# Two chunks' seeds in one pass, the last filter constants in a reused buffer, and new planner numbers, in an FFT convolution beside a Fourier mixing layer

## The chip, the cores and the metric

The kernel runs on one core of a Trainium2 chip. The core has a matrix engine (PE; its weight loads are listed as PEld), a vector engine (DVE), a scalar engine (ACT), a general engine (POOL) and an engine that here only issues DMAs (SP). The metric is the time of one execution in microseconds (us). Times inside the profile count from the first instruction of its span.

## The reference

Two independent layers read different inputs, and their outputs are put side by side, 2048 rows by 512 + 512 columns.

```python
# A: Fourier mixing, x is 2048 x 512
a = x @ dft_hid_re.T ; b = x @ dft_hid_im.T
ya = dft_seq_re @ a - dft_seq_im @ b
# B: a diagonal state space layer as a long convolution, u is 2048 x 512, 128 states for each of 512 channels
dt = exp(log_dt); A = -exp(log_A_real) + 1j * A_imag; C = (C_real + 1j * C_imag) * dt
K[d, l] = 2 * Re(sum_n C[d, n] * exp(A[d, n] * dt[d] * l))      # l = 0..2047
yb = causal_convolution(u, K) + u * D_skip                      # written with rfft / irfft of length 4096
```

## The kernel before: how the work is tiled and what sets its order

All instructions are recorded by Python generators, one for each piece of work. A small planner (`Plan`) keeps a time for each engine and records next whatever can start first by its own costs; between equals the smaller urgency number goes first. A `yield "dve", cost` in the code is one such piece; `Sem` and `Event` stand for buffers and for results. So a cost or an urgency in the code does not slow or speed anything by itself: it sets the order in which instructions stand in the engines' queues, and each engine then works its queue strictly in that order.

Layer A (class `Fnet`). The sequence matrices are streamed in as 32 quads ("S", 1 MB each, `load_quad`): a base tile and three others, which DVE combines into `rest` (L414), ACT squares for a guard value (L443) and PE multiplies (L520, L523). After each of four groups PE multiplies by the hidden matrices (L619, L620) and ACT and SP take `out_ya` away (L645, L648). `GROUP_US` and `QUAD_US` give the earliest planned time at which each quad may be asked for: "the pace of S". When the last quad is done, `spare` hands its two `slots` to layer B as further buffers.

Layer B (class `Ssm`), in stages that overlap:

- Seeds. For a chunk of 32 channels, `seed_args` makes 11 powers' exponents and angles: five small ACT copies (L993, L995), two DVE operations (L997, L999), then Abs, Exp and three Sin on ACT (L1001 to L1009). Exp and Sin live in different ACT tables, so each pass has ACT_TABLE_LOADs. `seeds` multiplies them on DVE (L1018) into the chunk's `cs` tile, of which there are two. The tile `seed` exists once.
- Tables. For each of the 16 chunks DVE doubles two tables of powers: `tables1` (T1, L944 and L953, 32 entries) and `tables2` (T2, L944 to L1110, with ACT squares in the tile `square`, L960, L967). This is most of DVE's work.
- Taps. PE multiplies the two tables into 96 numbers for each channel (`taps`, L1158), ACT moves them into `ks` (L1182).
- First FFT stage of K (`stage1_k`, L1234) for each two chunks, stored to DRAM in four tensors `xk`; the last two chunks (`last_stage1_k`, L1206) go to SBUF by DVE transposes (L1212) instead, with their own copy of the constants (`f1k_last`, L1283).
- Products. The channels fall into five units: 0, 1, 2 of 128 channels (four quarters each), 3 and 4 of 64 (two each). For a quarter, the spectra `xu` of u and `xk` of K are loaded from DRAM into a big buffer (L1367), PE does the second stage (L1399), ACT moves it out (L1424; unit 4: L1414), DVE multiplies (four operations, L1429 and L1431; unit 4: L1417), PE does the first inverse stage (L1445), ACT copies it (L808) and it is stored as `zs` (L796). Unit 3 is in `LATE`: its DVE products wait for chunk 15's T1 in the plan. Unit 4 stays in SBUF: four more transposes on DVE (L1496).
- Inverses. `zs` of a whole unit is loaded again (L1504), PE does the last stage (L1516), ACT or DVE copies, and `out_yb` is stored.

The buffers that products and inverses share are three `big` tiles, two `mid` tiles, later the two `slots`, and after chunk 15's tables the memory of the tables themselves (`more`). PE has four PSUM tiles (f0 to f3).

## Time and profile before

| what | value |
|---|---|
| three runs | 486.59, 488.81 and 490.38 us; median 488.81 |
| the profiled execution | 487.21 us |
| its span, first to last instruction | 485.10 us, so 2.11 us lie around it |
| busy in the span | PE 397.4, DVE 428.5, ACT 347.4 us |
| granted TensorE clock, mean | 0.961 |

A row of the timeline gives start, duration, engine, line and operation, out<-in, the shape and a count; a bracket says how long the engine stood idle just before and what ended that. "issue" in such a bracket means that nothing the profile shows was waited for. A row of the windows gives each engine's busy time in one stretch, then the granted clock, the share of the DMA engines and their rate. The end of T1 of a chunk is the end of its last L953.

### The profile page before, as it was taken

To read this page: it belongs to the slowest core of one execution; us is meant where nothing else is said; L and a number is where in the kernel's file an instruction comes from. 1 tells how busy PE (TensorE), PEld (TensorE's weight loads), DVE (VectorE), ACT (ScalarE), POOL (GpSimd) and SP (SyncE) were. 2 spreads that over 40 slices of the span, in tenths; PEclk is the share of its full clock that TensorE was granted. 3 is DMA by queue.
4 is the path that set the end of the run, shared out by engine and by line. 5 is a ranking of instruction groups with operands and counts; after the bars stand their busy time and mean duration, and the time that the engine had idled before them with its cause. 6 is when DMAs were issued, how large, how long until landed. Compare 5 with 4: busy or idle time off the path is not lost. (4 is left out here: it accounts for less than half of the span.)

```text
span 485.1 us, 13793 instructions
## 1 busy us (share of the span) xinstructions
PE 397.4 (82%) x5744; PEld 213.3 (44%) x5778; DVE 428.5 (88%) x732; ACT 347.4 (72%) x687; POOL 1.3 (0%) x15
## 2 busy tenths in 40 slices
PE   4548958999998695798897799998976989886593
PEld 3113214354534352453445254644343556665383
DVE  3999997989999999989999999999999999982433
ACT  1529899899998884669858988887897754633331
POOL 1000000000000000000000000000000000000000
PEclk9988987999999998999999999999999999997888
DMA  8998894895976379994986279449301995998674
GB/s 308 340 295 297 291 330 139 295 329 189 278 281 214 139 204 322 336 286 154 284 258 235 61 232 309 141 119 329 87 3 49 251 296 165 288 253 195 220 198 112
DMA packets 130546, 110.49 MB, mean 228 GB/s; under 512 B 57136, under 2 KB 101552, under 8 KB 129968
## 3 DMA queue, kind: packets, MB, share of 16 engines
q1 hardware_dynamic: 122512, 106.55, 70.1%
q10 hardware_dynamic: 7968, 3.02, 2.4%
q8 instruction: 47, 0.77, 0.7%
q14 instruction: 19, 0.16, 0.1%
HBM read 77.11 MB, written 32.44 MB: 226 GB/s over the span
## 5 line engine op out<-in xcount | busy, mean ns | idle before, releaser
L944 DVE TENSOR_TENSOR prod<-tables,cs 128x1024 f32<-128x1024 f32 (+4 forms) x160 | 124.6, 798 | 3.7 <-ACT tables L1087 2.3
L619 PE MATMUL f<-p,w 128*128 128x512 f32 x128 | 67.7, 610 | 8.9 <-ACT y L645 5.8
L953 DVE TENSOR_TENSOR tables<-prod 128x512 f32<-128x512 f32 (+4 forms) x160 | 74.0, 477 | 0.8
L443 ACT ACTIVATE slots<-rest 128x1536 f32<-128x1536 bf16 x32 | 47.4, 1480 | 16.3 <-DVE rest L414 13.8
L414 DVE TENSOR_TENSOR rest<-slots,base 128x512 bf16<-128x512 f32 (+2 forms) x52 | 53.8, 1034 | 1.9 <-DMA slots<-in_sT 1.8
L1158 PE MATMUL f<-tables 128*32 128x96 f32 x2048 | 47.0, 247 | 9.2 <-ACT big L808 2.8
L1158 PEld LDWEIGHTS f<-tables 128*32 128x32 f32 x2048 | 42.6, 110 | 18.6 <-issue 6.0
L520 PE MATMUL f<-base,es 128*128 128x512 f32 x64 | 36.9, 660 | 15.5 <-ACT es L331 7.2
L1110 DVE TENSOR_TENSOR tables<-tables,cs 128x1024 f32<-128x1024 f32 x32 | 38.0, 1220 | 0.0
L619 PEld LDWEIGHTS f<-p,w 128*128 128x128 f32 x128 | 22.5, 189 | 32.0 <-issue 16.0
L520 PE MATMUL f<-base,ec 128*128 128x512 f32 x64 | 34.3, 618 | 1.2 <-ACT big L1424 0.8
L523 PE MATMUL f<-rest,xi 128*128 128x512 bf16 x87 | 26.2, 397 | 5.7 <-ACT xi L273 2.5
L1399 PE MATMUL f<-big,w 64*32 64x256 f32 (+1 forms) x768 | 23.7, 380 | 6.1 <-DMA big<-xk 5.1
L1424 ACT ACTIVATE big<-f 128x1024 f32<-128x1024 f32 x22 | 21.9, 1020 | 7.8 <-PE f L1399 3.9
L808 ACT ACTIVATE big<-f 128x512 f32<-128x512 f32 x39 | 21.0, 588 | 7.2 <-PE f L1516 7.2
L523 PE MATMUL f<-rest,xr 128*128 128x512 bf16 x92 | 25.2, 379 | 0.6 <-DVE rest L414 0.4
L967 ACT ACTIVATE tables<-tables 128x1024 f32<-128x1024 f32 x16 | 16.8, 1050 | 10.5 <-PE f L1158 8.4
L1234 PE MATMUL f<-ks,f1k 32*128 32x512 f32 (+1 forms) x224 | 22.4, 499 | 2.3 <-ACT ks L1182 1.5
L523 PEld LDWEIGHTS <-xi 128*128 128x128 bf16 x96 | 9.5, 101 | 30.1 <-issue 21.8
L520 PEld LDWEIGHTS f<-base,es 128*128 128x128 f32 x64 | 11.8, 203 | 24.6 <-ACT es L331 10.5
L1023 ACT ACTIVATE cs<-cs 128x352 f32<-128x352 f32 x32 | 15.8, 530 | 9.0 <-DVE cs L1018 8.9
L1399 PEld LDWEIGHTS f<-big,w 64*32 64x32 f32 x768 | 14.0, 111 | 15.9 <-issue 10.6
(187 smaller groups left out, 732.7 us busy)
## 6 DMA issues: line engine op xcount, KB each, us to landing
slots<-in_sT SPq DMA_DIRECT2D x31, 768.0 KB, 6.0
xu<-big SPq DMA_DIRECT2D x16, 512.0 KB, 4.1
base<-in_sT SPq DMA_DIRECT2D x31, 256.0 KB, 6.2
xk<-big SPq DMA_DIRECT2D x7, 1024.0 KB, 6.8
big<-xu SPq DMA_DIRECT2D x11, 512.0 KB, 7.7
big<-xk SPq DMA_DIRECT2D x11, 512.0 KB, 7.3
zs<-mid SPq DMA_DIRECT2D x10, 512.0 KB, 6.2
big<-zs SPq DMA_DIRECT2D x10, 512.0 KB, 7.0
```

What stands on the lines that cost most here:

```text
L414: return v.tensor_tensor(rest[:, lo:hi:step], raw[:, lo:hi:step], base[:, None, :].to_broadcast([128, n, DM]), op=op)
L443: nc.scalar.activation(raw, rest, AF.Square, accum_out=self.stat[:, n:n + 1])
L520: nc.tensor.matmul(out, x[:, cols], base, start=k == 0, stop=False)
L523: nc.tensor.matmul(out, still[:, cols], rest[:, h], start=False, stop=k == 3 and h == 2)
L619: nc.tensor.matmul(ps, self.w[k][:, cols], self.p[t, c][:, d], start=k == 0, stop=False)
L944: self.nc.vector.tensor_tensor(p.rearrange("p k d c m -> p k (d c) m"), src.rearrange("p d c l -> p (d c) l")[:, None, :, rows].to_broadca ...
L953: self.nc.vector.tensor_tensor(dst[:, :, :, rows], p[:, 0], p[:, 1, :, ::-1], op=OP.add)
L1110: self.nc.vector.tensor_tensor(self.top[:, :, k, ::1 - 2 * k, 16:32], t[:, :, :, 1:32:2], cs[:, k, 5, :, :, None].to_broadcast([128, CHUNK ...
L1158: nc.tensor.matmul(ps[32 * j:32 * j + 32, i], t1[:, d, c], t2[:, :, d, c], start=c == 0, stop=c == 1, tile_position=(0, 32 * j))
L1234: nc.tensor.matmul(to, self.f1k[r, STEPS[a]], taps, start=a == 0, stop=a == 4, tile_position=(32 * j, 0))
L1399: nc.tensor.matmul(both[:, :, c], self.w2[rows, R * q + r, xx, 32 * c:32 * c + 32], xs[rows, r, xx], start=True, stop=True, tile_position= ...
L1424: a.activation(flat[:, 1024 * m:1024 * m + 1024], p.rearrange("p b d -> p (b d)"), AF.Copy)
```

## The change

1. Seeds are made for chunk 0 alone, for chunks 1 and 2, 3 and 4, ... 13 and 14 together, and for chunk 15 alone (`PAIRS`): nine passes in place of 16. A pass over two chunks has the same ten ACT operations and two DVE operations on 704 columns instead of 352. `seed` and the two `par` tiles become twice as large; the parameters of a pair come in one DMA (7 loads instead of 14 on SP). The DVE multiply into `cs` stays one for each chunk.
2. `f1k_last` no longer has its own 1.5 KB for each partition: it takes the tile `square`, and so its ACT copy waits for the new event `squared`, set after the last use of the squares in chunk 15's T2. The loads of unit 4's `xu` come behind that copy.
3. Numbers for the planner: urgency of the seeds 0.5 to 1.5 and of their arguments 0.3 to 1 (both still ahead of the tables' 2 and more, now behind taps and K stage with 0.5); taps cost 2.8 instead of 2.45; `GROUP_US` 42 to 41 and `QUAD_US` 11 to 8.
4. `spare` counts its buffers from `SLOTS`; with `SLOTS` = 2 it hands over the same one big and one mid tile.

```diff
-ARGS = 0.3
+ARGS = 1
...
+    def take_pair(self, g):
+        first, m = PAIRS[g]
+        self.pair[g] = self.tab.tile([128, 4, 2 * CHUNK], F32, name="par", bufs=2)[:, :, :m * CHUNK]
+        for j in range(m):
+            self.par[first + j] = self.pair[g][:, :, CHUNK * j:CHUNK * j + CHUNK]
...
-        self.par[ck] = self.tab.tile([128, 4, CHUNK], F32, name="par", bufs=2)
-        o = CHUNK * ck - FIRST
-        yield "dma", load(2 * CHUNK)
-        self.nc.sync.dma_start(self.par[ck], self.par_dram[:, :, o:o + CHUNK])
+        self.take_pair(g)
+        first, m = PAIRS[g]
+        o = CHUNK * first - FIRST
+        yield "dma", load(2 * m * CHUNK)
+        self.nc.sync.dma_start(self.pair[g], self.par_dram[:, :, o:o + m * CHUNK])
...
-        s = self.tab.tile([128, 3, 11, CHUNK], F32, name="seed")
+        s = self.tab.tile([128, 3, 11, 2 * CHUNK], F32, name="seed")[:, :, :, :w]
...
-        n = 11 * CHUNK
-        yield "act", 1.49
+        n = 11 * w
+        yield "act", 0.95 + 2 * n * 0.00085
...
-    def seeds(self, ck, s):
+    def seeds(self, g, j, s):
         yield self.css
+        s = s[:, :, :, CHUNK * j:CHUNK * j + CHUNK]
...
-        self.plan.put(self.res)
+        if j == PAIRS[g][1] - 1:
+            self.plan.put(self.res)
...
-        for n in range(16):
-            box, ev = args[n]
+        for g, (first, m) in enumerate(PAIRS):
+            box, ev = args[g]
             yield ev
-            if n < 15:
-                self.plan.spawn(self.seed_args(n + 1, *args[n + 1]), ARGS)
-            self.cs[n] = yield from self.seeds(n, *box)
-            self.plan.set(self.cs_ev[n])
+            if g < len(PAIRS) - 1:
+                self.plan.spawn(self.seed_args(g + 1, *args[g + 1]), ARGS)
+            for j in range(m):
+                self.cs[first + j] = yield from self.seeds(g, j, *box)
+                self.plan.set(self.cs_ev[first + j])
...
-            self.plan.put(self.pars)
+            if any(n == first + m - 1 for first, m in PAIRS):
+                self.plan.put(self.pars)
...
+            if n == 15:
+                self.plan.set(self.squared)
...
-            yield "pe", 2.45, None, 257
+            yield "pe", 2.8, None, 257
...
-        self.f1k_last = self.tab.tile([128, 3, 128], F32, name="f1k_last")
+        yield self.squared
+        self.f1k_last = self.tab.tile([128, 512], F32, name="square")[:, :384].rearrange("p (e s) -> p e s", e=3)
...
+PAIRS = ((0, 1), *((n, 2) for n in range(1, 15, 2)), (15, 1))
-FIRST_TABLE, T1, SEEDS = 0.01, 0.005, 0.5
+FIRST_TABLE, T1, SEEDS = 0.01, 0.005, 1.5
-GROUP_US, QUAD_US, AHEAD_US = 42, 11, 25
+GROUP_US, QUAD_US, AHEAD_US = 41, 8.0, 25
```

Since the planner's numbers change, nearly every queue is in another order. Three places matter below. Lines of the changed kernel are 12 to 20 higher: L944, L953, L1158, L1206, L1212, L1399, L1429, L1431, L1445 and L1516 of before are L956, L965, L1176, L1224, L1230, L1418, L1448, L1450, L1464 and L1535 after; L1367, L1504 and L796 are L1386, L1523 and L799.

First, DVE at the end of chunk 15's tables. Before, its queue reads (from the last steps of T2; the two rows of 128x32x16 on `tables<-prod` close the halves of T1 of chunk 15):

```order
L1106 SCALAR_TENSOR_TENSOR tables<-tables 128x32x16
L1110 TENSOR_TENSOR tables<-tables,cs 128x64x16
L1110 TENSOR_TENSOR tables<-tables,cs 128x32x2x16
L953 TENSOR_TENSOR tables<-prod 128x32x16
L944 TENSOR_TENSOR prod<-tables,cs 128x1024
L953 TENSOR_TENSOR tables<-prod 128x32x16
L1429 TENSOR_TENSOR mid_106<-slots 128x512
L1212 STREAM_TRANSPOSE tables<-f_4486 128x2x8x32
L1431 TENSOR_TENSOR slots<-slots 128x2x256
L1212 STREAM_TRANSPOSE tables<-f_4487 128x2x8x32
L1429 TENSOR_TENSOR mid_106<-slots 128x512
L1431 TENSOR_TENSOR slots<-slots 128x2x256
```

After, the corresponding stretch of the same queue starts a little ahead of T2's last step; ten rows with T1's smaller steps and two transposes (L1230) stand between its end and the second fence:

```order
L1448 TENSOR_TENSOR slots<-big_102 128x512
L1450 TENSOR_TENSOR big_102<-big_102 128x2x256
L1124 SCALAR_TENSOR_TENSOR tables<-tables 128x32x16
L1128 TENSOR_TENSOR tables<-tables,cs 128x64x16
L1128 TENSOR_TENSOR tables<-tables,cs 128x32x2x16
L956 TENSOR_TENSOR prod<-tables,cs 128x128
L965 TENSOR_TENSOR tables<-prod 128x64
L1448 TENSOR_TENSOR mid_105<-slots 128x512
L1450 TENSOR_TENSOR slots<-slots 128x2x256
L1448 TENSOR_TENSOR mid_105<-slots 128x512
L1450 TENSOR_TENSOR slots<-slots 128x2x256
```

```order
L956 TENSOR_TENSOR prod<-tables,cs 128x1024
L965 TENSOR_TENSOR tables<-prod 128x32x16
L1448 TENSOR_TENSOR mid_106<-big_103 128x512
L1450 TENSOR_TENSOR big_103<-big_103 128x4x128
L1448 TENSOR_TENSOR mid_106<-big_103 128x512
L1450 TENSOR_TENSOR big_103<-big_103 128x4x128
L1448 TENSOR_TENSOR slots<-big_104 128x512
L1450 TENSOR_TENSOR big_104<-big_104 128x4x128
L1448 TENSOR_TENSOR slots<-big_104 128x512
L1450 TENSOR_TENSOR big_104<-big_104 128x4x128
L1230 STREAM_TRANSPOSE tables<-f_4690 128x2x8x32
L1230 STREAM_TRANSPOSE tables<-f_4697 128x2x8x32
```

Moved: the products of unit 2's last two quarters (eight operations) and two of the four transposes now stand between the ends of T1 of chunk 14 and of chunk 15, before they stood behind; behind T1 of chunk 15 there now follow at once the products of unit 3.

Second, PE around chunk 15's taps (`L1158` / `L1176` x64 is one chunk). Before, from these taps on:

```order
L1158 MATMUL f_4527<-tables 32x96 x64
L1206 MATMUL f_4553<-ks,f1k_last 128x256 x2
L1206 MATMUL f_4588<-ks,f1k_last 128x256 x2
L1206 MATMUL f_4553<-ks,f1k_last 128x256 x2
L1206 MATMUL f_4588<-ks,f1k_last 128x256 x2
L1206 MATMUL f_4553<-ks,f1k_last 128x8x16 x2
L1206 MATMUL f_4588<-ks,f1k_last 128x8x16 x2
L1206 MATMUL f_4553<-ks,f1k_last 128x8x16 x2
L1206 MATMUL f_4588<-ks,f1k_last 128x8x16 x2
L1206 MATMUL f_4553<-dskip,f1k_last 128x8 x2
L1206 MATMUL f_4588<-dskip,f1k_last 128x8 x2
L1399 MATMUL f_4626<-big_103,w_95 32x2x128 x16
```

After, up to these taps (`L622` and `L623` are layer A's last products, before L619 and L620):

```order
L1418 MATMUL f_4612<-big_104,w_95 32x2x64 x32
L1418 MATMUL f_4613<-big_104,w_95 32x2x64 x32
L622 MATMUL f_4568<-p_3462,w_504 128x512
L623 LDWEIGHTS v_552
L623 MATMUL f_4568<-low_3497,v_552 128x512
L622 MATMUL f_4568<-p_3462,w_582 128x512
L623 LDWEIGHTS v_607
L623 MATMUL f_4568<-low_3497,v_607 128x512
L622 MATMUL f_4568<-p_3879,w_307 128x512
L623 LDWEIGHTS v_405
L623 MATMUL f_4568<-low_3897,v_405 128x512
L1176 MATMUL f_4615<-tables 32x96 x64
```

Moved: the second stage of unit 2's last quarter and of both quarters of unit 3 stood behind the last taps and now stands ahead of them; layer A's last products, which before were done ahead of the taps of chunk 14, now stand behind those: six pairs of them between the taps of chunks 14 and 15, three behind the taps of chunk 15.

Third, SP's queue of transfers near the end. Before (`xu` and `xk_86` 128x16x64 are the loads for units 3 and 4, `zs_89` is unit 2's store):

```order
L1367 DMA big_103<-xu 128x8x128
L1367 DMA big_103<-xk_85 128x8x128
L1367 DMA big_102<-xu 128x16x64
L1367 DMA big_102<-xk_86 128x16x64
L796 DMA out_yb<-big_104 128x4x128
L1367 DMA tables<-xu 128x16x64 x2
L1269 DMA tables<-in_ibl 128x2048
L1367 DMA tables<-xu 128x16x64
L1367 DMA tables<-xk_86 128x16x64
L796 DMA zs_89<-mid_106 128x8x128
L796 DMA zs_89<-slots 128x8x128
L1504 DMA big_104<-zs_89 128x1024 x2
```

After:

```order
L799 DMA xk_86<-big_104 128x2048
L799 DMA zs_89<-mid_106 128x8x128
L1386 DMA big_103<-xu 128x16x64
L1386 DMA big_103<-xk_86 128x16x64
L651 DMA out_ya<-y 128x512
L1386 DMA tables<-xu 128x16x64
L1386 DMA big_104<-xu 128x16x64
L1386 DMA big_104<-xk_86 128x16x64
L799 DMA zs_89<-slots 128x8x128
L1386 DMA tables<-xu 128x16x64
L799 DMA zs_89<-mid_105 128x8x128
L1523 DMA big_102<-zs_89 128x1024
```

Moved: both quarters of unit 3 are loaded into `big` tiles, ahead of unit 2's last stores; before, the second quarter (`tables<-xk_86`) waited for the tables' memory, behind the 1 MB load of `in_ibl`. The `big` tiles are free because unit 1's inverse loads (`zs_88`) and its `out_yb` stores now stand ahead of the loads for unit 2.

More of the change, by code (lines that the diff above doesn't have):

```diff
@@ L456, in spare @@
         flat = self.slots_all.rearrange("p n h t -> p (n h t)")
-        self.ssm.give_tile(self.ssm.big, flat[:, :2048])
-        self.ssm.give_tile(self.ssm.mid, flat[:, 2048:])
+        n = 3 * DM * SLOTS // 2048
+        for m in range(n):
+            self.ssm.give_tile(self.ssm.big, flat[:, 2048 * m:2048 * m + 2048])
+        for m in range(2 * n, 3 * DM * SLOTS // 1024):
+            self.ssm.give_tile(self.ssm.mid, flat[:, 1024 * m:1024 * m + 1024])
     def first(self):
@@ L736, in __init__ @@
         self.kss, self.res = Sem(1), Sem(1)
-        self.t1_half, self.half_taps, self.last_xt, self.last_k, self.last_ib = (Event() for _ in range(5))
+        self.t1_half, self.half_taps, self.last_xt, self.last_k, self.last_ib, self.squared = (Event() for _ in range(6))
         self.k_left = 2
@@ L845, in load_tables @@
         rest = part[4][:, :4 * (DM - FIRST)].rearrange("p (a d) -> p a d", a=4)
-        first = self.tab.tile([128, 4, CHUNK], F32, name="par", bufs=2)
+        first = self.tab.tile([128, 4, 2 * CHUNK], F32, name="par", bufs=2)[:, :, :CHUNK]
         yield self.pars
+        self.pair = {0: first}
         self.rest, self.par = rest, {0: first}
@@ L913, in setup_rest @@
         yield self.pars
-        self.par[1] = self.tab.tile([128, 4, CHUNK], F32, name="par", bufs=2)
-        yield "act", act(4 * CHUNK)
-        self.nc.scalar.activation(self.par[1], par[:, :, :CHUNK], AF.Copy)
+        self.take_pair(1)
+        yield "act", act(8 * CHUNK)
+        self.nc.scalar.activation(self.pair[1], par[:, :, :2 * CHUNK], AF.Copy)
         self.plan.set(self.par1_ev)
@@ L1001, in seed_args @@
         a.activation(k, r, AF.Abs)
-        yield "act", 1.74
+        yield "act", act(n) + 1.36
         a.activation(e, e, AF.Exp, scale=-1.0)
-        yield "act", 1.57
+        yield "act", act(6 * w) + 1.32
         a.activation(r[:, 0:6], r[:, 0:6], AF.Sin, scale=TWO_PI)
-        yield "act", act(5 * CHUNK)
+        yield "act", act(5 * w)
         a.activation(r[:, 6:11], r[:, 6:11], AF.Sin, scale=-TWO_PI)
@@ L1031, in tables @@
         yield from self.setup()
-        args = [([], Event()) for _ in range(16)]
+        args = [([], Event()) for _ in PAIRS]
         self.plan.spawn(self.seed_args(0, *args[0]), ARGS)
```

14 lines of the change are left out of this document (7 added, 7 removed).

## The prediction

> **What bounds the kernel now.** I read the busy totals first, then the windows by stage, what DVE waited for, and last the timelines of DVE, PE and SP near the end. The totals of the page:
>
> ```profile
> PE 397.4 (82%) x5744; PEld 213.3 (44%) x5778; DVE 428.5 (88%) x732; ACT 347.4 (72%) x687; POOL 1.3 (0%) x15
> q8 instruction: 47, 0.77, 0.7%
> ```
>
> DVE is the fullest engine, but the windows say where. They are cut at the ends of T1 of chunk 14 (call it T14) and of chunk 15 (T15); the columns are PE, PEld, DVE, ACT and POOL busy, then the granted clock:
>
> ```profile
> 60.00:140.00 80.00, 71.64 (x610) 31.48 (x612) 75.09 (x132) 76.11 (x152) 0.00 (x0) 0.94 0.80 263
> 140.00:412.09 272.09, 234.56 (x3395) 125.25 (x3421) 263.27 (x457) 211.90 (x418) 0.00 (x0) 0.99 0.66 204
> 412.09:425.78 13.69, 11.65 (x372) 8.69 (x368) 13.35 (x21) 8.37 (x15) 0.00 (x0) 1.00 0.98 281
> 425.78:485.10 59.32, 40.56 (x1256) 32.20 (x1256) 25.79 (x36) 18.78 (x31) 0.00 (x0) 0.86 0.74 195
> ```
>
> From 60 us to T14 DVE is idle for 4.9 + 8.8 = 13.7 us of 352: there the time is DVE's work. In the last 59.3 us DVE is 43% busy and PE 68%: no engine is full, a chain is long. So two numbers decide: T14, and the 485.1 - 412.1 = 73.0 us behind it. DVE's longest waits:
>
> ```profile
> DVE prod L1429 <- ACT tables L1424: 10.1, 1, 10.1
> DVE prod L944 <- ACT tables L1087: 2.3, 1, 2.3
> ```
>
> The first is in the tail, the second the longest between 60 us and T14. DVE's timeline gives the marks:
>
> ```profile
> 411.42 0.67 DVE L953 TENSOR_TENSOR tables<-prod 128x512 f32<-128x512 f32 x1
> ...
> 425.09 0.69 DVE L953 TENSOR_TENSOR tables<-prod 128x512 f32<-128x512 f32 x1
> ...
> 430.10 2.07 DVE L1212 STREAM_TRANSPOSE tables<-f 128x512 f32<-128x512 f32 x2
> ```
>
> T14 is 411.42 + 0.67 = 412.09, T15 is 425.09 + 0.69 = 425.78. PE's timeline, with the price of each step that I use:
>
> ```profile
> 401.25 1.13 PE L619 MATMUL f<-p,w 128*128 128x512 f32 x2
> 402.21 0.38 PE L620 MATMUL f<-low,v 128*128 128x512 bf16 x1
> 402.52 1.96 PE L1399 MATMUL f<-big,w 64*32 64x256 f32 x64
> ...
> 415.22 2.85 PE L1158 MATMUL f<-tables 128*32 128x96 f32 x128
> ...
> 428.33 1.61 PE L1206 MATMUL f<-ks,f1k_last 32*128 32x256 f32 x32 [0.67 <-ACT ks L1182]
> ...
> 431.89 1.23 PE L1445 MATMUL f<-slots,ia 32*64 32x256 f32 x26
> ...
> 434.13 0.85 PE L1399 MATMUL f<-big,w 64*32 64x128 f32 x39
> ...
> 442.11 1.56 PE L1445 MATMUL f<-slots,ia 32*64 32x256 f32 x21 [3.69 <-issue]
> ...
> 447.44 2.59 PE L1399 MATMUL f<-tables,w 64*32 64x128 f32 x165
> ...
> 457.72 2.00 PE L1445 MATMUL f<-prod,ia 32*64 32x256 f32 x28 [2.92 <-issue]
> 460.45 1.98 PE L1516 MATMUL f<-big,ib 128*64 128x128 f32 x16 [0.73 <-ACT prod L808]
> 462.36 3.08 PE L1399 MATMUL f<-tables,w 64*32 64x128 f32 x128
> ...
> 469.42 1.18 PE L1445 MATMUL f<-tables,ia 32*64 32x256 f32 x32
> ```
>
> A pair of layer A's products takes 402.52 - 401.25 = 1.3 us, a first inverse stage 434.13 - 431.89 = 2.2. Unit 3's second quarter, out of the tables' memory, comes only at 447.44; unit 4's last second stage at 462.36; its last first inverse stage starts at 469.42, and from there copies, transposes, last stage and store take 485.10 - 469.42 = 15.7 us to the end.
>
> **The change part by part.** Sums are made against the profiled execution's 487.21 us (span 485.10); the median of the runs is 1.60 us higher, which I add at the end.
>
> *Seeds in pairs, ACT.* Rows by shape, and a wide copy as the price of a wide operation:
>
> ```profile
> L1005 ACT ACT_TABLE_LOAD x16 | 20.5, 1283 | 0.2
> L1003 ACT ACT_TABLE_LOAD x15 | 19.2, 1283 | 0.3
> L1003 ACT ACTIVATE seed<-seed 128x352 f32<-128x352 f32 x16 | 7.9, 497 | 0.2
> L1182 ACT ACTIVATE ks<-f 128x768 f32<-128x768 f32 x8 | 6.4, 797 | 0.5 <-PE f L1158 0.5
> ```
>
> ACT's queue has 18 table loads in place of 32: 14 x 1.283 = 18.0 us less. Seven passes of ten operations go, and one twice as wide costs at most 0.80 instead of 2 x 0.50: about 0.2 x 70 = 14 us more. ACT falls from 347 to about 315 us. DVE's work covers this: ACT's relief shows only where DVE waited, so the ends are 0 and -13.7; I take 0, since no wait of DVE there is above 2.3 us. The Trainium skill (ScalarE: Activation LUTs, "What ACT_TABLE_LOAD costs") gives 2.66 us for a switch with its drain. By that ACT would be spared 37 us by the switches alone; the rows show 1.283 us and no drain.
>
> *Seeds in pairs, DVE.*
>
> ```profile
> L999 DVE TENSOR_TENSOR seed<-seed x16: 511/520/527, 41.0 to 378.6; 128x352 f32<-128x352 f32 x16
> L1018 DVE TENSOR_TENSOR cs<-seed x16: 885/890/899, 50.2 to 388.4; 128x704 f32<-128x704 f32 x16
> ```
>
> At 704 columns L999 costs what L1018 does, 0.89 instead of 1.04; for L997 I take the same saving. 7 x 0.30 = 2.1 us, half of it if only the overlap-free part counts. I take -1.5, all on the path to T14.
>
> *Seeds less urgent, par loads.* `seed` exists once: a pair's arguments start when the pair before is multiplied out, and then have about a chunk's time (366 us from 60 to T15 for 16 chunks, 23 each) for ten ACT operations of at most 0.8 us and two loads, 10.6 us. So I take 0; ends 0 and +5 (half a microsecond of hungry DVE in each pass). SP's seven par loads less are hidden by the same slack.
>
> *DVE between T14 and T15.* Eight product operations and two transposes are added here (first order fences):
>
> ```profile
> L1431 DVE TENSOR_TENSOR big<-big 128x512 f32<-128x512 f32 x22 | 15.2, 692 | 1.5
> L1212 DVE STREAM_TRANSPOSE tables<-f 128x512 f32<-128x512 f32 x4 | 4.2, 1092 | 0.0
> ```
>
> 8 x 0.69 + 2 x 1.09 = 7.7, less overlap about 7.2. T15 goes from T14 + 13.7 to T14 + 20.9; the second added transpose ends some 6 us ahead of that, at + 15.
>
> *PE behind T14.* Its new queue, in us from T14: taps of chunk 14 to 2.9, a pair of layer A 4.2, unit 2's last second stage 6.2, a first inverse stage 8.4, L1206 (1.9 with its small rows) 10.3, unit 3's first quarter (2.3) 12.6. The next first inverse stage needs the PSUM tiles of the two transposes: 15 to 17.2. Two pairs 19.8, unit 3's second quarter 22.1, three pairs 26.0, taps of chunk 15 28.9. So T15 is not on the path any more: PE comes five microseconds later. Copy into `ks`, a pair and L1206 to 32, transposes to 34; unit 3's two first inverse stages, with a pair between, to 39; its copies and an inverse piece (1.0) to 41; unit 4's first quarter (2.6, between 2.0 and 3.1) 43.7, two inverse pieces 45.7, its second quarter 48.4; an inverse piece, a first inverse stage and unit 3's inverse (1.2) to 52.8. There unit 4's last first inverse stage starts, 15.7 us before the end: 68.5.
>
> *Pauses.* PE's pauses marked "issue" are in none of these steps; before, they cost 3.69 and 2.92 in the stretch where unit 2's and 3's steps stood close. 47 pieces of code serve 5744 + 5778 = 11,522 instructions, about 250 each, and the new stretch is as dense. I take +2, ends 0 and +7. The Trainium skill (Runtime: NRT & Kernel Launch, "Instruction fetch mechanics") says that crossing a block of 256 instructions is mostly hidden. By that this term would be 0; the two pauses speak against it.
>
> So 73.0 us become 70.5: -2.5, ends -4.5 and +2.5. Most of what unit 3 gains by its `big` tiles is paid back by layer A's nine pairs (11.5 us) that now stand behind T14.
>
> *The wait for `squared`.* Behind the ACT copy stand the copies of unit 2's last product. The squares are used up 3 us behind T14, as the taps end, and that product comes at 6.2: 0, at most 1 without this cover.
>
> *The pace of S* gave these places; by itself I put 0, between -3 and +3.
>
> Sum: 485.1 - 1.5 - 2.5 = 481.1, with 2.1 around it 483.2, and 1.6 for the median: **484.8 us**.
>
> **Rivals.** *C, ACT's relief counts.* If half of DVE's 13.7 us of idle time goes, T14 and the end come 7 us earlier: 478. For it: ACT is 95% busy in 60:140, and DVE idles there. Against: the waits are many and short.
>
> *A, pauses and round trips eat the rest.* Unit 2's spectrum goes through DRAM before its inverse, and PE's queue stands behind that inverse.
>
> ```profile
> 445.24 0.36 SPq L796 DMA_DIRECT2D zs<-slots  x1
> 450.41 1.69 SPq L1504 DMA_DIRECT2D slots<-zs  x2
> ```
>
> Before, from the last store (445.24) to the inverse (460.45) it took 15.2 us. Now the store is due at T14 + 18.5, its loads behind an `out_ya` store that waits for layer A's pairs (+26.5): the inverse may come at +45 instead of +40. 484.8 + 5 = 490, no change.
>
> *B, slower: the last K spectrum comes late.* Unit 3's products now stand ahead of chunk 15's taps in PE's queue. If `xk_86` has not landed, PE stops, and all behind it.
>
> ```profile
> 414.27 0.33 SPq L796 DMA_DIRECT2D xk<-big  x1
> xk<-big SPq DMA_DIRECT2D x7, 1024.0 KB, 6.8
> big<-xk SPq DMA_DIRECT2D x11, 512.0 KB, 7.3
> ```
>
> Before, the product ran 434.13 - 414.27 = 19.9 us after the store was issued, at T14 + 22.0. Now PE is there at + 10.3; landing at + 22 would cost 12: 497 us. Against it: the K stage stands two stages, three pairs (8 us) ahead of chunk 14's taps in the new queue, so its copies (3), store and load are done by T14 + 9. It makes the change slower by over 1% from a landing at T14 + 20 on.
>
> **How the numbers follow.** My forecast (480 to 489) has 0.50, C 0.20, A 0.16, B 0.14. Within 1% of the median, about what a measurement of this kernel can tell from no change, is 484 to 494. Faster: C and under half of the forecast, 0.42; same: the rest of it and A, 0.43; slower: B and an edge, 0.15. The range 474 to 496 leaves out the lower part of C and the upper half of B.
>
> **What would show it.** DVE near full up to T14, and T14 between 408 and 413; ACT near 315 us with 17 or 18 table loads; no DMA wait of PE at unit 3's second stage; chunk 15's taps some 5 us behind T15; 68 to 73 us from T14 to the end. A T14 below 406 would be C, a wait for `zs` at L1535 A, a DMA wait at L1418 ahead of the taps B.

## The result and the profile after

| | before | changed |
|---|---|---|
| median of 20 runs, us | 488.96 (485.45 to 492.97) | 485.76 (482.87 to 494.11) |
| profiled execution, us | 487.21 | 486.11 |
| its span, us | 485.10 | 484.30 |
| granted TensorE clock, mean | 0.961 | 0.937 |

The ratio changed / before is 0.9937, 95% interval 0.9909 to 0.9965: 0.6% faster, within the 1% named as "same". Ratios here and below are taken over undisturbed runs alone, so they need not equal the quotient of the medians, which are over all runs.

The totals of the changed kernel's page, and the rows of its ACT table loads:

```profile
PE 403.1 (83%) x5737; PEld 212.0 (44%) x5778; DVE 426.8 (88%) x718; ACT 320.9 (66%) x603; POOL 1.3 (0%) x15
```

```profile
L1017 ACT ACT_TABLE_LOAD x9 | 11.5, 1283 | 0.1
L1015 ACT ACT_TABLE_LOAD x8 | 10.3, 1283 | 0.1
```

ACT lost 26.6 us and has 17 of these loads left (and one at L331). DVE lost 1.7. PE is 5.7 us busier for the same 5778 weight loads, at a lower granted clock. The marks on DVE's timeline (start, duration; T14 ends with the first of the two operations of the first row):

```profile
409.77 1.02 DVE L965 TENSOR_TENSOR tables<-prod 128x512 f32<-128x512 f32 x2
...
431.01 0.69 DVE L965 TENSOR_TENSOR tables<-prod 128x512 f32<-128x512 f32 x1
```

So T14 is about 410.45 and T15 is 431.70. The windows cut there:

```profile
60.00:140.00 80.00, 72.94 (x608) 32.02 (x612) 74.30 (x121) 69.28 (x126) 0.00 (x0) 0.91 0.81 267
140.00:410.45 270.45, 234.40 (x3557) 125.30 (x3587) 262.19 (x449) 193.50 (x360) 0.00 (x0) 0.96 0.72 213
410.45:431.70 21.25, 17.87 (x579) 12.21 (x569) 20.52 (x32) 12.15 (x16) 0.00 (x0) 1.00 1.00 216
431.70:484.30 52.60, 35.84 (x897) 26.04 (x890) 19.02 (x27) 13.05 (x25) 0.00 (x0) 0.88 0.55 153
```

DVE's idle time from 60 us to T14 is 5.70 + 8.26 = 14.0 us (13.7 before), although ACT has 26.6 us less to do. T14 came 1.6 us earlier. Behind it lie 73.85 us (73.0 before). PE's timeline there:

```profile
409.30 2.85 PE L1176 MATMUL f<-tables 128*32 128x96 f32 x128
...
423.20 0.65 PE L1418 MATMUL f<-big,w 64*32 64x128 f32 x26 [1.56 <-issue]
...
429.80 2.03 PE L1418 MATMUL f<-big,w 64*32 64x128 f32 x128
...
436.13 1.53 PE L1176 MATMUL f<-tables 128*32 128x96 f32 x64
...
451.18 1.09 PE L1535 MATMUL f<-big,ib 128*64 128x128 f32 x16 [1.46 <-ACT slots L811]
...
466.17 1.15 PE L1535 MATMUL f<-tables,ib 128*64 128x64 f32 x32 [2.39 <-DMA tables<-zs]
467.25 1.12 PE L1464 MATMUL f<-tables,ia 32*64 32x256 f32 x32
...
471.52 1.98 PE L1535 MATMUL f<-tables,ib 128*64 128x64 f32 x32 [2.29 <-issue]
474.67 1.97 PE L1535 MATMUL f<-big,tables 128*64 128x64 f32 x32 [1.18 <-issue]
```

Unit 3's second quarter (429.80) waits for no DMA, and chunk 15's taps (436.13) come 4.4 us behind T15. Late in the tail PE waits 2.39 us for unit 3's spectrum, which went through DRAM. ACT's queue, and then SP's, show that round trip (ACTq and SPq rows are DMA issues):

```profile
449.18 1.25 ACTq L799 DMA_DIRECT2D zs<-mid  x1
450.53 1.09 ACT L811 ACTIVATE slots<-f 128x512 f32<-128x512 f32 x2 [2.30 <-DMA out_ya<-y]
451.65 3.01 ACTq L799 DMA_DIRECT2D zs<-slots  x1
```

```profile
461.26 0.79 SPq L1523 DMA_DIRECT2D tables<-zs  x2
```

The second store alone held ACT for 3.01 us.

The two last inverse pieces in PE's timeline (474.67 and 477.33) read what DVE transposes. The transposes end at 470.16 + 4.41 = 474.57, and PE starts 0.10 us later; before, they end at 476.82 and PE starts at 476.92, and in e5, e6, e10 and x2 (below) it is 0.10 us too. So the mark "issue" at this row stands for a wait for DVE, not for nothing. The transposes after and before, and PE's row before:

```profile
470.16 4.41 DVE L1515 STREAM_TRANSPOSE big<-tables 128x512 f32<-128x512 f32 x4
```

```profile
472.37 4.45 DVE L1496 STREAM_TRANSPOSE big<-tables 128x512 f32<-128x512 f32 x4
```

```profile
476.92 1.15 PE L1516 MATMUL f<-big,tables 128*64 128x64 f32 x32 [1.65 <-issue]
```

The last stretch, from unit 4's last first inverse stage on, cut where PE starts the first of these two pieces, after and then before:

```profile
467.25:474.67 7.42, 3.96 (x99) 3.19 (x97) 5.10 (x5) 1.79 (x3) 0.00 (x0) 0.78 0.42 106
474.67:484.30 9.63, 3.94 (x64) 3.57 (x64) 0.69 (x1) 0.60 (x1) 0.00 (x0) 0.50 0.43 86
```

```profile
469.42:476.92 7.50, 5.16 (x147) 4.42 (x145) 5.14 (x5) 3.00 (x6) 0.00 (x0) 1.00 0.50 132
476.92:485.10 8.18, 2.30 (x64) 2.02 (x64) 0.69 (x1) 0.60 (x1) 0.00 (x0) 0.79 0.44 110
```

The first part is as long as before, and PE's pause of 2.29 us lies inside it, ahead of a piece that is done before the transposes are. The second is 1.45 us longer: at a granted clock of 0.50 each of its two pieces takes 1.97 us, before 1.15. Four more traces with PE's queue in this order (e1, e6, e12, x2, below) have 1.97 or 1.98 there too; e7, with the queue of before, and e10 have 1.15; e4, also with the queue of before, has 1.15 and 1.83. Why the clock was lower there was not tried.

### The profile page after: what moved, and what is told of

Its sections match the earlier page's. It is cut to its first block, busy times and chain, and to the rows that moved or that the text cites. A ratio compares the mean times of both kernels' runs of the same rounds, so it can differ in the third digit from the quotient of the medians.

```text
span 484.3 us, 13684 instructions
## 1 busy us (share of the span) xinstructions
PE 403.1 (83%) x5737; PEld 212.0 (44%) x5778; DVE 426.8 (88%) x718; ACT 320.9 (66%) x603; POOL 1.3 (0%) x15
## 5 line engine op out<-in xcount | busy, mean ns | idle before, releaser
L956 DVE TENSOR_TENSOR prod<-tables,cs 128x1024 f32<-128x1024 f32 (+4 forms) x160 | 124.1, 798 | 3.1 <-ACT tables L1103 1.2
L965 DVE TENSOR_TENSOR tables<-prod 128x512 f32<-128x512 f32 (+4 forms) x160 | 73.1, 477 | 0.9
L622 PE MATMUL f<-p,w 128*128 128x512 f32 x128 | 69.9, 628 | 3.9 <-ACT y L648 3.4
L1176 PE MATMUL f<-tables 128*32 128x96 f32 x2048 | 48.6, 250 | 8.0 <-issue 5.6
L1176 PEld LDWEIGHTS f<-tables 128*32 128x32 f32 x2048 | 43.7, 111 | 17.7 <-issue 11.5
L523 PE MATMUL f<-base,es 128*128 128x512 f32 x64 | 40.1, 712 | 12.7 <-DMA big<-in_x 6.3
L622 PEld LDWEIGHTS f<-p,w 128*128 128x128 f32 x128 | 22.7, 193 | 28.3 <-issue 18.9
L1418 PE MATMUL f<-big,w 64*32 64x256 f32 (+1 forms) x896 | 26.0, 370 | 7.1 <-DMA big<-xk 5.2
L1443 ACT ACTIVATE big<-f 128x1024 f32<-128x1024 f32 x24 | 23.7, 1022 | 9.6 <-PE f L1418 9.6
L811 ACT ACTIVATE mid<-f 128x512 f32<-128x512 f32 x24 | 13.0, 590 | 17.1 <-PE f L1464 17.1
L972 ACT ACTIVATE square<-tables 128x256 f32<-128x256 f32 (+1 forms) x32 | 16.6, 518 | 10.7 <-DVE tables L965 10.5
L1418 PEld LDWEIGHTS f<-big,w 64*32 64x32 f32 x896 | 15.9, 111 | 17.2 <-issue 9.8
```

Source lines behind the costliest of these rows:

```text
L523: nc.tensor.matmul(out, x[:, cols], base, start=k == 0, stop=False)
L622: nc.tensor.matmul(ps, self.w[k][:, cols], self.p[t, c][:, d], start=k == 0, stop=False)
L811: self.nc.scalar.activation(to, src, AF.Copy)
L956: self.nc.vector.tensor_tensor(p.rearrange("p k d c m -> p k (d c) m"), src.rearrange("p d c l -> p (d c) l")[:, None, :, rows].to_broadca ...
L965: self.nc.vector.tensor_tensor(dst[:, :, :, rows], p[:, 0], p[:, 1, :, ::-1], op=OP.add)
L1176: nc.tensor.matmul(ps[32 * j:32 * j + 32, i], t1[:, d, c], t2[:, :, d, c], start=c == 0, stop=c == 1, tile_position=(0, 32 * j))
```

## The experiments

Every span can be split as 60 us + DVE's busy time from there to T15 + its idle time in that stretch + the time behind T15. The split, from the windows of each profiled execution, for the kernels on seeds and order (us; ratios are to the kernel before):

| kernel | DVE busy | DVE idle | behind T15 | span | ratio, 95% interval |
|---|---|---|---|---|---|
| before | 351.71 | 14.07 | 59.32 | 485.10 | 1 |
| changed | 357.02 | 14.68 | 52.60 | 484.30 | 0.9937, 0.9909 to 0.9965 |
| e1, ACT's old work | 357.88 | 34.93 | 53.59 | 506.40 | 1.0448, 1.0394 to 1.0502 |
| e12, only 14 loads back | 359.52 | 30.51 | 52.37 | 502.40 | 1.0358, 1.0306 to 1.0410 |
| e9, old work, planned | 359.04 | 24.05 | 58.51 | 501.60 | 1.0310, 1.0271 to 1.0349 |
| e2, pairs, old numbers | 358.14 | 19.59 | 52.37 | 490.10 | 1.0047, 1.0010 to 1.0084 |
| e10, pairs, new urgencies only | 357.74 | 17.10 | 48.46 | 483.30 | 0.9926, 0.9895 to 0.9956 |
| e3, single seeds, new numbers | 359.21 | 17.76 | 48.83 | 485.80 | 1.0008, 0.9984 to 1.0033 |
| x1, layer A's outputs early | 357.91 | 20.29 | 47.60 | 485.80 | 0.9993, 0.9958 to 1.0028 |

The first two rows say where the work went: DVE's idle time is about the same, some 5 us of product work moved ahead of T15 (more of DVE ahead, less behind), and the time behind T15 is 6.7 us shorter. In sum that is 0.8 us of span, where the ratio says 3.1: each row is one execution. How far executions of one order lie apart is seen in runs whose queues up to T14 are the same. DVE's idle time is 14.07, 15.72 and 12.04 us in three with the order of before (before, e4, e7) and 12.56 to 14.68 in four with the new one (changed, e5, e6, x2), so a difference of 2 or 3 us in this column shows nothing by itself. T14 is 409.95, 412.09 and 414.91 in the three, 408.85 to 410.45 in the four. The time from T14 to the end is 73.0 us before and 73.4 in e4, 73.85 in the changed kernel and 74.0 in x2.

**e1: ACT's old work in the new order.** All queues but ACT's keep the changed kernel's rows.

```diff
...
-        a.activation(k, r, AF.Abs)
+        for x in halves:
+            a.activation(k[:, :, x], r[:, :, x], AF.Abs)
         yield "act", act(n) + 1.36
-        a.activation(e, e, AF.Exp, scale=-1.0)
+        for x in halves:
+            a.activation(e[:, :, x], e[:, :, x], AF.Exp, scale=-1.0)
+            if x is not halves[-1]:
+                a.activation(r[:, 0:6, x], r[:, 0:6, x], AF.Sin, scale=TWO_PI)
...
```

`halves` holds one slice of 32 columns for each chunk of the pass.

> The changed kernel, but ACT works each pair's two chunks apart again: copies, Abs, Exp and three Sin on 352 columns for the first chunk, then for the second. The queues of PE, DVE and SP hold the same rows in the same order as the changed kernel's; ACT alone has the old work back: 32 table loads and about 347 us busy instead of 321. My theory (until T14 the time is DVE's work, and ACT's relief is worth nothing on the path): 0 to +2 us against the changed kernel, so a ratio of 0.992 to 0.998 to the kernel before; DVE's idle time from 60 us to T14 stays at 14 to 16 us. Rival C (ACT's relief is what made the gain): +3 to +13 us, the ratio at or above 1.000, and DVE's waits for ACT grow by as much.

Measured: 509.49 us, ratio 1.0448, about 25 us above the changed kernel. ACT is at 348.6 us, so 27.7 us more of ACT cost nearly as much in time. My theory was off by an order of magnitude, and rival C's range was too small too. DVE's waits in this kernel (total, times, longest; L972 is a square and L1111 a copy of T2, both on ACT):

```profile
DVE tables L991 <- ACT square L972: 14.4, 6, 3.8
...
DVE prod L956 <- ACT tables L1111: 7.7, 3, 3.4
```

In the changed kernel:

```profile
DVE prod L956 <- ACT tables L1103: 1.2, 1, 1.2
DVE tables L991 <- ACT square L972: 0.5, 1, 0.5
```

Together the two waits grew by 20.4 us, and DVE's idle time by 20.25. Short ACT work that stands in its queue behind or among the seeds comes late.

**e12: only the table loads back.** Exp and the first Sin for each chunk of a pair apart, the rest wide.

```diff
+        x = slice(0, CHUNK)
+        if w > CHUNK:
+            a.activation(e[:, :, x], e[:, :, x], AF.Exp, scale=-1.0)
+            a.activation(r[:, 0:6, x], r[:, 0:6, x], AF.Sin, scale=TWO_PI)
+            x = slice(CHUNK, w)
-        a.activation(e, e, AF.Exp, scale=-1.0)
+        a.activation(e[:, :, x], e[:, :, x], AF.Exp, scale=-1.0)
         yield "act", act(6 * w) + 1.32
-        a.activation(r[:, 0:6], r[:, 0:6], AF.Sin, scale=TWO_PI)
+        a.activation(r[:, 0:6, x], r[:, 0:6, x], AF.Sin, scale=TWO_PI)
```

> The changed kernel, but in each of the seven pair passes only the Exp and the first Sin are done for each chunk apart, in the order Exp, Sin, Exp, Sin: 14 table loads come back (32 in all), and 14 narrow operations. That is 2.9 us more of ACT in each pass, about 20 us in all, in the same place of its queue; all other queues hold the changed kernel's rows in its order. The experiment with all of ACT's old work added 27.7 us to ACT and about 25 us to the time. Theory S (in the changed kernel's order ACT's seed pass has no slack, so its time comes through nearly whole): +14 to +19 us against the changed kernel, a ratio of 1.022 to 1.033. Theory D (a pass has a slack of some 2 us, and only what lies above it counts): +2 to +9 us, 0.998 to 1.012.

Measured: 506.2 us, ratio 1.0358, 20.6 us above the changed kernel (0.0421 x 488.96), for 20.9 us more of ACT (341.7 against 320.9). That is theory S, at or a little above its upper end (the interval starts at 1.0306): by the ratios, give or take 3 us, nothing of ACT's added time is hidden; by the two profiled spans 18.1 of the 20.9 us come through. DVE's same two waits:

```profile
DVE tables L991 <- ACT square L972: 11.0, 6, 3.1
DVE prod L956 <- ACT tables L1108: 6.0, 3, 2.7
```

They grew by 15.3 us, DVE's idle time by 15.8. One pass shows how. In the changed kernel ACT works without a pause from the pass's Abs to its last Sin, and T2's first copy (L1103) stands among them:

```profile
245.47 0.80 ACT L1013 ACTIVATE seed<-seed 128x704 f32<-128x704 f32 x1 [0.78 <-DVE seed L1011]
...
254.68 0.30 ACT L1103 ACTIVATE tables<-cs 128x64 f32<-128x64 f32 x1
...
255.50 0.87 ACT L1021 ACTIVATE seed<-seed,halfpi 128x704 f32<-128x704 f32 x1
257.73 0.60 ACT L811 ACTIVATE big<-f 128x512 f32<-128x512 f32 x1 [1.37 <-PE f L1535]
```

DVE reads what L1103 writes without waiting (the second of the two operations in this row; there is no bracket):

```profile
254.09 1.51 DVE L956 TENSOR_TENSOR prod<-tables,cs 128x1024 f32<-128x1024 f32 x2
```

With two more loads in the pass, the same copy (now L1108) comes 3.0 us later behind the Abs, and DVE stands still for 2.68 us:

```profile
256.64 0.79 ACT L1013 ACTIVATE seed<-seed 128x704 f32<-128x704 f32 x1 [0.78 <-DVE seed L1011]
...
268.85 0.30 ACT L1108 ACTIVATE tables<-cs 128x64 f32<-128x64 f32 x1
...
269.66 0.86 ACT L1026 ACTIVATE seed<-seed,halfpi 128x704 f32<-128x704 f32 x1
```

```profile
269.18 0.40 DVE L956 TENSOR_TENSOR prod<-tables,cs 128x128 f32<-128x128 f32 x1 [2.68 <-ACT tables L1108]
```

**e9: ACT's old work, but planned.** Each narrow operation is a piece of its own, with its cost, so the order is made anew (here also for PE, DVE and SP).

```diff
...
+        for x in halves:
...
+            yield "act", 1.74
+            a.activation(e[:, :, x], e[:, :, x], AF.Exp, scale=-1.0)
+            yield "act", 1.57
+            a.activation(r[:, 0:6, x], r[:, 0:6, x], AF.Sin, scale=TWO_PI)
...
```

> As the experiment before with ACT's old work (32 table loads, narrow operations, each chunk's Exp and Sin apart), but each of these operations is now a piece of its own with its own cost in the plan, so the planner puts squares and other short ACT work between them and the order is made for the longer ACT. Theory L (what cost 22 us was a lump of about 6 us that stands in ACT's queue ahead of squares for which DVE waits, where the order reckoned with 2): the ratio falls to 0.995 to 1.008 and DVE's idle time from 60 us to T15 to 15 to 22 us, from 35. Theory T (ACT's time itself bounds the tables once products and tables stand this close): the ratio stays above 1.025 and the idle time above 28 us.

Measured: 503.98 us, ratio 1.0310; idle 24.05 us, between the two forecasts; the time behind T15 is 5.9 us longer in the order that came out. In the ratio theory T holds. Re-ordering wins back 11 of the 20 us that e1 added to DVE's idle time, no more. Since e3 has the same work on ACT (348.0 us) with 17.76 us of idle time, it is not ACT's total alone. My reading, from the code and not from a run of its own: `seed` exists once, so a pair's pass has to be done between one chunk's seeds and the next, and with the old loads and narrow operations it is twice a single pass there.

**e2, e10, e3: pairs and planner numbers apart.** e2 is the changed kernel with all numbers of before, e10 with only the taps costs and the pace of before, e3 the kernel before with all the new numbers. The edits of e2 and e10, shortened:

```diff
 e2:  -ARGS = 1            +ARGS = 0.3
      -SEEDS 1.5           +SEEDS 0.5
 e2 and e10:
      -taps 2.8 and 1.42   +taps 2.45 and 1.25
      -pace 41 and 8.0     +pace 42 and 11
```

> The changed kernel with all the planner's numbers of before (seeds 0.5, arguments 0.3, taps 2.45 and 1.25, pace 42 and 11): pairs and the reused buffer alone. My theory (the gain is 1.5 us of DVE work up to T14, and the rest the order behind T14, in which unit 3 runs from big tiles): T14 at 410 to 412; the order behind T14 puts unit 3 behind chunk 15's taps and takes unit 4 from the tables' memory late, much as before, so the tail is 72 to 76 us and the ratio 0.995 to 1.003. Rival N (the pairs alone make the gain, and the numbers do nothing): 0.991 to 0.996, as the changed kernel.

> The changed kernel with the planner's taps costs (2.45 and 1.25) and pace of before, but the new urgencies of the seeds; the pace by itself changes no place in any queue. If the seeds' urgencies are what the pairs need: 0.990 to 0.996, as the changed kernel. If the taps cost is what put unit 3 ahead of chunk 15's taps: 1.000 to 1.006, as with all the old numbers, which gave 1.0047. DVE's idle time from 60 us to T15 (14.7 us in the changed kernel, 19.6 with all the old numbers) and the tail behind T15 (52.6 and 52.4 us) say which part it is.

> The kernel before with only the planner's new numbers (seeds 1.5, arguments 1, taps 2.8 and 1.42, pace 41 and 8): single seeds, 32 table loads, its own f1k_last. My theory: T14 where it was, 411 to 414 (the seeds' slack is enough also for single chunks), and a tail like the changed kernel's, 73 to 75 us, so a ratio of 0.996 to 1.006. Rival N2 (the numbers alone make the gain): 0.991 to 0.996. A third possibility: less urgent single seeds come late for hungry DVE in each chunk; then T14 moves to 416 or later and the ratio is above 1.008.

Measured: e2 490.68 us (1.0047), e10 484.86 us (0.9926), e3 489.5 us (1.0008). So neither pairs with the old numbers nor single seeds with the new ones gain anything, and pairs with the new urgencies gain as much as the whole change. My forecast for e2's ratio just missed at its upper end, and its T14 is 421.4, not 410 to 412. Against the changed kernel that is 10.9 us, of which 5.5 are more work of DVE ahead of T14 (products that moved there) and 5.4 more idle time. So T14 is no fair mark between orders, and the split at T15 is used. e3's ratio is as forecast, but its T14 (418.5) is 6.4 us later than before, 2.9 of them work and 3.5 idle time: that half of the third possibility came. The tails behind T14 are 68.7 us in e2 and 67.3 in e3, below the 72 to 76 and 73 to 75 forecast. For e10 the first of the two possibilities holds. The time behind T15 is no different in e2 than in the changed kernel; its 4.9 us more of DVE's idle time are. For each of the three the order of all queues differs, so a few tenths of a per cent can belong to the order that came out and to no single number. The pace needs no run: with 42 and 11 in the changed kernel every queue holds the same rows in the same places.

**e4: f1k_last in the squares' tile, alone, in the kernel before.** The queues keep their rows.

```diff
...
+            if n == 15:
+                self.plan.set(self.squared)
...
+        yield self.squared
-        self.f1k_last = self.tab.tile([128, 3, 128], F32, name="f1k_last")
+        self.f1k_last = self.tab.tile([128, 512], F32, name="square")[:, :384].rearrange("p (e s) -> p e s", e=3)
```

> The kernel before with only f1k_last in the squares' tile, and so behind the event that the squares are used up. My theory: 0, at most +1 us (0.998 to 1.002). Rival: ACT stands at the copy and holds what is queued behind it, or the loads of unit 4's xu come too late: +2 us or more (1.004 and above), with a wait of ACT at that copy of over 1 us.

Measured: 489.15 us, ratio 1.0035, 0.9995 to 1.0074: too wide to tell 0 from +2 us. The trace has no idle time of ACT ahead of this copy, so the wait that the rival needs is not there; nor does PE wait for a load behind T15.

**e5: layer A's last nine pairs cut short.** Their fp32 product is left out.

```diff
-                nc.tensor.matmul(ps, self.w[k][:, cols], self.p[t, c][:, d], start=k == 0, stop=False)
-                nc.tensor.matmul(ps, self.v[k][:, cols], self.low[t, c][:, d], start=False, stop=k == 3)
+                short = t == 3 and 4 * e + k > 6
+                if not short:
+                    nc.tensor.matmul(ps, self.w[k][:, cols], self.p[t, c][:, d], start=k == 0, stop=False)
+                nc.tensor.matmul(ps, self.v[k][:, cols], self.low[t, c][:, d], start=short and k == 0, stop=k == 3)
```

> The changed kernel without the fp32 product of layer A's last nine pairs, all behind chunk 14's taps in PE's queue (the bf16 product of each pair stays; these parts of the first output are not computed). Some 8.6 us of PE's work are gone from the stretch behind T14. My theory (the chain behind T14 is PE's queue, and these pairs pay back most of unit 3's gain): chunk 15's taps start at T14 + 22 instead of + 25.7, held by T15 at + 21.3, one more pair is gone from ahead of unit 3's inverses, and the end comes 4 to 5.5 us earlier, a ratio of 0.982 to 0.987. Rival (a round trip through DRAM or waits for ACT set the end): at most 1 us, 0.991 to 0.996.

Measured: 484.31 us (479.30 to 487.69, six runs), ratio 0.9841, 0.9790 to 0.9893: by the ratio the theory (4.7 us off the changed kernel, about 2 to 7.5 by the intervals), by the medians about 1 us, and in the profiled run (span 483.5) 0.8 us. Six runs that spread over 8.4 us don't settle it. The profiled run shows where its gain went. PE, ACT and DVE in it:

```profile
444.76 1.09 PE L1537 MATMUL f<-big,ib 128*64 128x128 f32 x16 [0.89 <-ACT slots L813]
...
452.22 1.98 PE L1537 MATMUL f<-big,ib 128*64 128x128 f32 x16 [4.41 <-ACT big L813]
...
474.38 1.80 PE L1537 MATMUL f<-big,tables 128*64 128x64 f32 x32 [4.32 <-issue]
```

```profile
445.22 6.30 ACTq L801 DMA_DIRECT2D zs<-slots  x1
451.57 0.60 ACT L813 ACTIVATE big<-f 128x512 f32<-128x512 f32 x1 [6.38 <-issue]
```

```profile
469.94 4.34 DVE L1517 STREAM_TRANSPOSE big<-tables 128x512 f32<-128x512 f32 x4
```

PE is at the first inverse piece at 444.76 where the changed kernel was at 451.18, 6.4 us ahead. Chunk 15's taps start at 431.84, right behind T15 at 431.56, as forecast. Then the issue of unit 3's second store holds ACT for 6.30 us (3.01 in the changed kernel), PE waits 4.41 us for ACT's copy, its granted clock falls to 0.58 in the next 6.4 us, and when it reaches unit 4's last first inverse stage, at 466.30, it is only 1.0 us ahead of the changed kernel. (The 4.32 us at the end are the wait for the transposes, which end at 474.28.) So the pairs stand on PE's path up to the first inverse piece; that the end comes as much earlier is not shown.

**e6 and e7: more DVE work ahead of T15**, in the changed kernel and in the one before.

```diff
             yield from self.add(p, t[:, d], to)
+            for _ in range(3 if ev else 0):
+                self.nc.vector.tensor_tensor(t[:, d, :, to], p[:, 0], p[:, 1, :, ::-1], op=OP.add)
```

> The changed kernel with 4.1 us more work of DVE between T14 and T15: the additions that close the two halves of chunk 15's T1 are each done three times more (six operations of 0.69 us; the result is the same). My theory (T15 is off the path, PE comes to chunk 15's taps 4.4 us behind it): 0 to +1.5 us, a ratio of 0.993 to 0.997. Rival (T15 still decides): +3 to +4 us, 1.000 to 1.003.

> The same 4.1 us more of DVE's work in chunk 15's T1, in the kernel before, where PE stood 0.86 us at chunk 15's taps until DVE had closed T1. My theory (there T15 is on the path): +3 to +4.1 us, a ratio of 1.006 to 1.009. Rival (T15 was off the path before too): 0 to +1, up to 1.002.

Measured: e6 486.95 us, ratio 0.9955 (0.9921 to 0.9989), 0.9 us above the changed kernel; e7 492.18 us, ratio 1.0110 (1.0074 to 1.0147), 5.4 us above the kernel before. Both as the theory has it, e7 a little more. The profiled executions are less clear. In e7's the span is only 1.4 us longer, since T14 came 2.1 us earlier there; from T14 to the end it is 3.5 us. In e6's, T14 to the end is 3.7 us longer too, but there PE's pauses marked "issue" ahead of the taps, all in the middle of a stage, make 5.2 us (1.9 in the changed kernel). So the finding rests on the runs and on PE's rows at chunk 15's taps, first e6 (line 1178), then e7 (line 1160):

```profile
437.72 1.13 PE L622 MATMUL f<-p,w 128*128 128x512 f32 x2 [0.69 <-ACT y L648]
...
438.99 1.53 PE L1178 MATMUL f<-tables 128*32 128x96 f32 x64
```

```profile
423.98 2.47 PE L1160 MATMUL f<-tables 128*32 128x96 f32 x64 [3.32 <-DVE tables L1055]
428.14 2.79 PE L1160 MATMUL f<-tables 128*32 128x96 f32 x64 [1.69 <-DVE tables L1055]
```

In e6 the taps follow a pair with no wait; in e7 PE stands for DVE twice.

**x1 and x2: two tries for a faster version.** x1 makes layer A's last group more urgent, x2 moves unit 3's stores, of its spectrum and of out_yb, from ACT's to SP's queue. (One out_yb store of unit 4 goes from SP to ACT with it, near the end, which the expectation has otherwise.)

```diff
 x1: -FNET, ... = (2.0, 2.0, 2.0, 2.0)   +FNET, ... = (2.0, 2.0, 2.0, 0.9)
 x2: -LATE_Z 3                           +LATE_Z 4
```

> The changed kernel with the urgency of layer A's last group at 0.9 instead of 2.0: all 16 of its last pairs now stand ahead of chunk 12's taps in PE's queue, none behind T14. The order of the other queues changes with it. My theory (the nine pairs behind T14 cost about 4.6 us of the tail, and PE has room ahead of T14): T14 at 410 to 416, the tail behind T15 47 to 51 us, a ratio of 0.983 to 0.994. Rival (PE and ACT have no room there: the pairs and their copies hold up taps, products and the squares that DVE waits for): DVE's idle time from 60 us to T15 rises by 5 us or more, and the ratio is 0.997 or above.

> The changed kernel with unit 3's two stores of its spectrum, and the three out_yb stores that stood in ACT's queue (unit 3's and unit 4's first halves), as SP issues them in the same places of the plan; the queues of PE and DVE hold the same rows. In the changed kernel's trace the second of these stores holds ACT 3.01 us, and PE waits 2.39 us for the spectrum ahead of unit 4's last first inverse stage. My theory (this round trip is on the path): 1 to 3 us less, a ratio of 0.987 to 0.992. Rival (SP's queue makes up for it, since the stores stand behind others there, or the chain behind is ACT's copies): within 1 us of the changed kernel, 0.992 to 0.996.

Measured: x1 488.98 us, ratio 0.9993, the rival: the time behind T15 fell by 5.0 us to 47.6, as the theory said, and DVE's idle time rose by 5.6. x2 485.36 us, ratio 0.9939 (0.9906 to 0.9973), the rival: within measurement the changed kernel. Its SP queue, and PE:

```profile
451.10 5.74 SPq L799 DMA_DIRECT2D zs<-slots  x1
...
460.69 1.08 SPq L1523 DMA_DIRECT2D tables<-zs  x2
```

```profile
465.34 1.15 PE L1535 MATMUL f<-tables,ib 128*64 128x64 f32 x32 [1.57 <-DMA tables<-zs]
```

ACT is free, but the store takes 5.74 us on SP, the loads are issued only 0.6 us earlier, and PE still waits 1.57 us. No version tried beats the changed kernel by more than the measurement can tell; e10, at 0.9926, is level with it.

## Why the prediction was right, and where it was not

The forecast was 484.8 and the median is 485.76, but in part by luck. The steps forecast a span of 481.1 us, 4.0 less than before; the profiled executions have 484.30, 0.8 less. What made up for it is the 1.6 us by which the profiled execution before stood below its median: the one after stood 0.35 above its own. By the forecast's own steps:

- *Seeds in pairs, ACT: worth 0 on the path.* The sum was right within what one execution tells: DVE's idle time to T14 went from 13.7 to 14.0. The reason was wrong. "DVE's work covers this" means that ACT had slack, and e1 and e12 show that in the changed order it has none: 20.9 us of ACT cost 20.6, give or take 3. What I put in its place is a reading: a pair's pass is twice as long and must fit where a single pass did, and the spared loads and fixed costs about pay for that. In its favour: with as much ACT work e1 and e9 stand 22 and 15 us above e3, which has single seeds. The term would then be a difference of two large amounts, not a small effect under cover. The forecast for ACT's total, 315, measured 320.9: the loads gave the 18.0 us, the narrow operations 8.6 instead of 14.
- *Seeds in pairs, DVE: -1.5.* DVE's total fell by 1.7. T14 came 1.6 us earlier, which is within the spread of T14 over executions of one order.
- *Seeds less urgent: 0.* Together with pairs this number does matter: from all the old numbers (e2) to the new urgencies (e10) the ratio falls by 0.0121, 5.9 us. In the profiled spans DVE's idle time falls by 2.5 us, no more than executions of one order differ, and the time behind T15 by 3.9.
- *DVE between T14 and T15:* + 20.9 forecast, + 21.25 measured. *T15 off the path:* right, by 4.4 us; the runs of e6 (0.9 us above the changed kernel, give or take 2) and of e7 show it from both sides.
- *PE behind T14:* this is the step that failed, -2.5 forecast and +0.85 measured (x2 and e4 have 74.0 and 73.4 us behind T14, which says the same). The end lies outside the 68 to 73 us named as a sign. Most places were right: taps of chunk 15 at + 25.7 (26.0 forecast), the first inverse piece at + 40.7 (39 to 41). (One place is a slip: 34 and two stages with a pair between make 39.7, not 39.) Two parts of the sum were too small. Unit 4's last first inverse stage starts at 467.25, + 56.8, where 52.8 and the 2 us of pauses made 54.8: the sum knew no round trip of unit 3's spectrum, for which PE waits 2.39 us right ahead of this stage. That is rival A's mechanism, at unit 3 and not at unit 2, and of 2.39 us and not 5. And from there to the end it took 17.05 and not 15.7: the two last inverse pieces at the granted clock of 0.50.
- *Pauses: +2.* Those marked "issue" in the changed kernel up to 467.25, all in the middle of a stage of PE, are 0.38, 1.56 and 0.85 us, together 2.79.
- *Most of unit 3's gain is paid back by the nine pairs:* in e5 they stand on PE's path as far as the first inverse piece, but what their leaving out is worth at the end stays unsettled; x1 shows that they cannot be moved for nothing: ahead of T14 they cost DVE what they free behind.
- *Wait for `squared`: 0*; no run contradicts it. *Pace of S: 0*: in the changed kernel it moves no row in any queue.
- *Rival C* fell as it was put: ACT's relief did not shorten DVE's idle time. *Rival B* did not come about: no wait for a DMA ahead of chunk 15's taps.

Open: where the 3.1 us of the ratio lie, since the profiled pair shows 0.8 of them, and how much of the 0.6% is the order's luck. e2, e3, e10 and x1 differ in the order of all queues and spread over 1.2%.

## What to carry to other kernels

"Off the critical path" is a statement about an engine's total; it does not say that a longer block in that engine's queue is free. Before costing a relief at nothing, ask how long the new block is, and which short instructions for the bounding engine stand behind it in the same queue. To test it, put the old cost back under the new order: that separates the relief from the reordering, which comparing two orders cannot.

## What the runs showed of the hardware that was not expected

- The issue of a store to DRAM can hold the issuing engine for long: the second half of unit 3's spectrum (512 KB) took 3.01 and 6.30 us on ACT and 5.74 on SP, the first half 1.25 us on ACT in the changed kernel. On ACT the next copy starts as the issue ends (451.57 where the issue ran from 445.22 to 451.52). The cause was not tried; a 1 MB load is issued on SP at about the same time.
- A table load took its 1283 ns here, and no drain is seen beside it: in e12 14 loads and 14 narrow operations made ACT 20.9 us busier and the kernel 20.6 us longer, give or take 3, and each of its four groups of seed loads has 0.1 us of idle time or less ahead of it in all. The Trainium skill (ScalarE: Activation LUTs, "What ACT_TABLE_LOAD costs") gives 2.66 us for a switch with its drain; by that figure 14 switches alone are an estimate of 37 us, which this time excludes.
- The granted clock was 0.50 in the last 9.63 us of the changed kernel, and the same inverse piece took 1.97 us there and 1.15 before. The mean over the span (0.937) doesn't show it; a window over the last stretch does.
